# One accumulator row, two copies and five late weight pieces at the end of a decode-attention kernel

## Chip, cores and metric

The kernel runs on one core of a Trainium2 chip. The metric is device time in microseconds (us) for one execution; lower is better. Before the change three runs took 1010.38, 1010.63 and 1011.29 us, median 1010.63.

## What is computed

One query token attends to two caches, and a gate mixes the two results. All data is float32.

```python
def attention(x, k, v, wq, wo):          # x: [1, 448]; 16 query heads of 256; 8192 positions
    q = (x @ wq).reshape(16, 256)
    p = softmax(einsum("hd,hkd->hk", q, k) * 256 ** -0.5)
    return einsum("hk,hkd->hd", p, v).reshape(1, 4096) @ wo      # [1, 448]

g = sigmoid((x * gate_w).sum(-1))
out = g * attention(x, A_k, A_v, A_wq, A_wo) \
    + (1 - g) * attention(x, repeat(B_k, 2), repeat(B_v, 2), B_wq, B_wo)
```

A has 16 key/value heads, B has 8, each serving two query heads. The caches make up nearly all of the 432 MB that the kernel reads.

## The kernel before

**The stream.** The host lays all inputs into one array, `stream`, in the order in which they are used. `plan()` writes this order: a list of fills, each a list of loads, each a list of pieces (kind, number, offset, columns). A ring of three SBUF slots takes the fills in turn, and the loop at the end of the kernel issues the loads on SP's queue (L469) and calls `piece` for each piece. Most fills are one load of 7936 KB. The last ones are cut finer by hand: the last key/value tiles, then the last tile of values in three loads (`LAST_CUT`, 8, 4 and 4 rows), then the last set's output weights `wo` in four loads: 448 KB (head 3), 448 KB (head 0), 672 KB (head 1 and half of head 2), 224 KB (the other half of head 2).

**The work.** There are eight sets (`s` from 0 to 7). A set is three units: unit 2 is a B head with its two query heads, units 0 and 1 are two A heads. A unit is four tiles of 2048 positions. TensorE computes scores of units 2 and 1 (`scores`, L255); VectorE computes those of unit 0 (`scores_by_row`, L277 and L281). ScalarE takes the exponentials, and TensorE multiplies with the values (`attend`, L307). At a unit's end ScalarE and VectorE merge the two halves of its accumulator (`take`, L316 and L317), `combine` and `column` make its softmax weights (L337 to L366), and `project_o` (L372, copy L374) turns the result into columns.

**The output.** `YY[0]` is a PSUM tile that collects the output. For sets 0 to 6 `emit_set` (L381) multiplies each of the four heads of a set with its wo and adds it to row 0, 32, 64 or 96 by head, 448 columns wide. After set 6 `fold` copies the tile to SBUF (L387), takes a new one, clears it (L186) and sums the four rows into it (L391) by a column `any4` that has ones at these rows: from here on row 32g holds columns 112g to 112g + 111. `emit` (L398) adds a head of the last set in this form: two halves of the head (`e`) times four column blocks (`g`), eight matmuls of 112 columns. In the trace a float32 matmul is two instructions.

**The end.** The order is written out after the loop: project the last unit, (s, 1), then `emit` for (s, 2) head 0, (s, 1), (s, 2) head 1 and (s, 0), as the four wo loads come. VectorE copies rows by 112 columns (L483), and SP stores four pieces of 448 bytes (L484). The schedule is manual: each engine runs its instructions in the order of the program, and the framework sets the semaphores.

Of the kernel before, what the change touches and what calls it, by code (L numbers as in the profile page):

```python
# [7 lines left out]
F32 = mybir.dt.float32  # L8
BF16 = mybir.dt.bfloat16
AF = mybir.ActivationFunctionType  # L10
# [4 lines left out]
P = 128  # L15
D = 448
# [3 lines left out]
KF = D // P  # L20
KR = D - KF * P
NG = 4
YN = D // NG

NS = 8
ROWS = 16
# [10 lines left out]
BY_ROW = {(s, 0) for s in range(NS)}  # L37
LAST_CUT = [8, 4, 4]
HEAD_AT = {2: 0, 0: 2, 1: 3}
TILES = [((s, r), t) for s in range(NS) for r in UNITS for t in range(NT)]  # L40


# [4 lines left out]
def plan():  # L47

    size = {"xg": XG, "k": ROWS * DH, "v": ROWS * DH, "wq": WQ, "wo": 8 * D}
    per = len(UNITS) * NT  # L50
    n = len(TILES)
    items = []
    for i in range(n + LEAD):
        if i == 0:
            items += [("xg", 0), ("wq", 0)]
        if i < n:
            items.append(("k", i))
        if i >= LEAD:
            items.append(("v", i - LEAD))
        if i % per == 7 and i // per + 1 < NS:  # L60
            items.append(("wq", i // per + 1))
        if i % per == LEAD + 1 and i >= per:
            items.append(("wo", i // per - 1))
    loads, room = [[]], FULL
    last = [("v", n - 3), ("v", n - 2)]
    for kind, i in items[:items.index(last[0])]:
        at, left = 0, size[kind]
        while left:
            step = min(left, room) // ATOM[kind] * ATOM[kind]
            if step:  # L70
                loads[-1].append((kind, i, at, step))
            at, left, room = at + step, left - step, room - step * (kind != "xg")
            if left:
                loads.append([])
                room = FULL

    loads = [[x] for x in loads]
    x = loads[-2][0]
    loads[-2] = [x[:2], x[2:]]
    loads[-1] += [[(kind, i, 0, size[kind])] for kind, i in last]  # L80
    at, end = 0, []
    for c in LAST_CUT:
        end.append([("v", n - 1, at, c * DH)])
        at += c * DH

    for h, e, n in ((3, 0, 2), (0, 0, 2), (1, 0, 3), (2, 1, 1)):
        end.append([("wo", NS - 1, (2 * h + e) * D, n * D)])
    return loads + [end]


LOADS = plan()


@with_exitstack
def kernel(
# [5 lines left out]
    nc = tc.nc  # L101
    scale = DH ** -0.5

    const = ctx.enter_context(tc.tile_pool(name="const", bufs=1))
# [5 lines left out]
    ps_y = ctx.enter_context(tc.tile_pool(name="ps_y", bufs=1, space=PSUM))  # L110
# [3 lines left out]
    def heads(u):  # L114
        return 2 if u[1] == 2 else 1
# [35 lines left out]
    any4 = const.tile([P, 1], F32, name="any4")  # L151
# [33 lines left out]
    def clear(t, n):  # L185
        nc.tensor.matmul(t[:, :n], zero, zero[:, None, :n // 4].to_broadcast([P, 4, n // 4]), start=True, stop=False, skip_group_check=True)  # L186


    YY = [ps_y.tile([P, D], F32, name="Y")]
# [17 lines left out]
    ST, PR, O, GS, WR, SEL, OB, OC = ({} for _ in range(8))  # L207
# [103 lines left out]
    def take(u):  # L311

        o = O.pop(u)
        ob1 = small.tile([P, DH], F32, name="ob1", bufs=1)
        OB[u] = small.tile([P, DH], F32, name="ob", bufs=3)
        nc.scalar.activation(ob1, o[:, DH:], AF.Copy, scale=half[:, 1:2])  # L316
        nc.vector.scalar_tensor_tensor(OB[u], o[:, :DH], half[:, 0:1], ob1, op0=OP.mult, op1=OP.add)  # L317
# [50 lines left out]
    def project_o(u):  # L368
        M = heads(u)
        oc = ps_s.tile([P, 2, 2], F32, name="sm")  # L370
        for e in range(2):
            nc.tensor.matmul(oc[:, e, :M], OB[u][:, e::2], SEL[u][:, :M], start=True, stop=True)  # L372
        ocs = small.tile([P, 2, 2], F32, name="ocs", bufs=4)
        nc.vector.tensor_copy(ocs[:, :, :M], oc[:, :, :M])  # L374
        OC[u] = ocs
# [8 lines left out]
    def fold():  # L384

        yf = small.tile([P, NB * BLK], F32, name="px")
        nc.scalar.activation(yf[:, :D], YY[0], AF.Copy)  # L387
        YY[0] = ps_y.tile([P, D], F32, name="Y")
        clear(YY[0], YN)
        for g in range(NG):  # L390
            nc.tensor.matmul(YY[0][32 * g:32 * g + 1, :YN], any4, yf[:, g * YN:(g + 1) * YN], start=False, stop=False,  # L391
                             skip_group_check=True)

    def emit(u, m, last=False):
        for e in range(2):
            wt = LAST[HEAD_AT[u[1]] + m, e]
            for g in range(NG):
                nc.tensor.matmul(YY[0][32 * g:32 * g + 1, :YN], OC[u][:, e, m:m + 1], wt[:, g * YN:(g + 1) * YN],  # L398
                                 start=False, stop=(last and e == 1), skip_group_check=True)


    LAST, GW = {}, {}
# [3 lines left out]
    def wait(n, f, *args):  # L406
        todo.append([n, f, args])

    def tick():
        for t in todo:  # L410
            t[0] -= 1
        for t in [t for t in todo if t[0] <= 0]:
            todo.remove(t)
            t[1](*t[2])

    def piece(kind, i, at, view):
# [14 lines left out]
        elif kind == "k":  # L431
            u, t = TILES[i]
            if u in BY_ROW:
# [10 lines left out]
        elif kind == "v":  # L444
            u, t = TILES[i]
            n = view.shape[-1] // DH
            attend(u, t, at // DH, n, view.rearrange("p (j d) -> p j d", d=DH))
            if at // DH + n == ROWS:
                if t == NT - 1:
                    take(u)  # L450
                    if u != TILES[-1][0]:
                        wait(1, project_o, u)
                if i >= len(TILES) - LEAD:
                    tick()
        elif kind == "wo" and i < NS - 1:
            emit_set(i, j0, view.rearrange("p (c n) -> p c n", c=n))
            if i == NS - 2 and j0 + n == 8:
                fold()
        else:
            for j in range(n):  # L460
                LAST[divmod(j0 + j, 2)] = view[:, j * D:(j + 1) * D]

    off = 0
    for fill in LOADS:
        buf = ring.tile([P, FULL + XG], F32, name="slot")
        c = 0
        for load in fill:
            n = sum(x[3] for x in load)
# [4 lines left out]
                c += x[3]  # L473
    assert not todo
    s = NS - 1
    project_o((s, 1))
    emit((s, 2), 0)
    emit((s, 1), 0)
    emit((s, 2), 1)
    emit((s, 0), 0, last=True)  # L480

    ys = const.tile([P, YN], F32, name="ys")
    nc.vector.tensor_copy(ys, YY[0][:, :YN])  # L483
    nc.sync.dma_start(out.rearrange("a b (g n) -> (a b g) n", g=NG), ys[::32, :])  # L484


_OUTS = [((1, 1, D), "float32")]
# [64 lines left out]
```

## Time and profile before

| what | value |
|---|---|
| median of three runs | 1010.63 us |
| profiled execution | 1010.95 us |
| its span, first to last instruction | 1009.2 us |
| TensorE matmul busy | 578.0 us (57%) |
| VectorE busy | 465.1 us (46%) |
| read from HBM | 432.02 MB, 428 GB/s over the span |
| mean granted TensorE clock | 0.773 |

The span is what the profiler saw of the program; the execution's time is 1.8 us longer. In the profile PE is TensorE's matmuls, PEld its weight loads, DVE VectorE, ACT ScalarE, SP the queue that issues the loads. Times in the trace are counted from the span's start. PEclk is the TensorE clock granted, as a share of 2.4 GHz; it is 1.00 or 0.50 at any moment. A share of busy time is an average over the span; what a change at the end is worth is read from the last microseconds.

### The profile page before, as it was taken

How to read it: one execution, taken by the hardware profiler on the slowest of the kernel's cores; microseconds unless marked ns; L12 is line 12 of the kernel's file. 1: busy time of each engine (PE TensorE's matmuls, PEld its weight loads, DVE VectorE, ACT ScalarE, POOL GpSimd, SP SyncE). 2: the span in 40 equal slices, each digit the busy share in tenths (PEclk: the TensorE clock that was granted, in tenths of full speed). 3: DMA queues.
4: the chain of work that ended last, by engine and by line, in shares of the span. 5: the costliest groups of instructions: out<-in, count | busy, mean ns of one | idle time of the engine just before them, and what ended most of it. 6: DMA issues, size and time to landing. Idle time of an engine off the chain costs nothing.

```text
span 1009.2 us, 7624 instructions
## 1 busy us (share of the span) xinstructions
PE 578.0 (57%) x3154; PEld 169.8 (17%) x3154; DVE 465.1 (46%) x732; ACT 90.0 (9%) x267; POOL 1.9 (0%) x10
## 2 busy tenths in 40 slices
PE   0846745565745655636646556645656537537557
PEld 0211211121211111112111111111211112111112
DVE  1486213961248521576215841248521585216851
ACT  0100100010100110001100001100110000101010
POOL 0000000000000000000000000000000000000000
PEclk9977877767777887867787777776886777777788
DMA  9999999999999999999999999999999999999997
GB/s 403 439 438 425 431 436 439 435 421 433 439 436 425 436 431 441 431 428 433 441 428 429 438 431 433 435 431 438 431 431 426 440 438 426 428 433 441 424 421 299
DMA packets 9114, 432.50 MB, mean 429 GB/s; under 512 B 1016, under 2 KB 1144, under 8 KB 1784
## 3 DMA queue, kind: packets, MB, share of 16 engines
q1 hardware_dynamic: 9080, 432.02, 99.1%
q8 instruction: 24, 0.39, 0.2%
q14 instruction: 10, 0.08, 0.0%
HBM read 432.02 MB, written 0.00 MB: 428 GB/s over the span
## 4 chain that ended last, share of the span: by engine, by line
DMA 71%; PE 14%; DVE 12%; ACT 2%; issue 1%; ACTq 0%; SPq 0%; DVEq 0%
DMA slot<-in_stream_dram 71%; PE o L307 6%; PE sc L255 5%; DVE sr L281 4%; DVE slot L277 4%; PE sm L220 2%; ACT px L264 1%; DVE mn L261 1%; DVE pr L267 1%; PE sm L237 0%; DVE pr L294 0%; ACT pxr L290 0%; ACT ew L345 0%; PE sm L361 0%; DVE st L262 0%
## 5 line engine op out<-in xcount | busy, mean ns | idle before, releaser
L307 PE MATMUL o<-slot,pr 128*32 128x512 f32 (+1 forms) x1536 | 349.9, 758 | 224.6 <-DMA slot<-in_stream_dram 224.6
L255 PE MATMUL sc<-slot,qb 128*32 128x512 f32 x1024 | 197.5, 715 | 104.7 <-DMA slot<-in_stream_dram 101.7
L261 DVE TENSOR_REDUCE mn<-sc 128x1 f32<-128x512 f32 x64 | 44.1, 690 | 325.7 <-PE sc L255 300.9
L277 DVE TENSOR_TENSOR slot<-slot,qa 128x4096 f32<-128x4096 f32 (+7 forms) x40 | 142.6, 3565 | 41.1 <-DMA slot<-in_stream_dram 41.0
L307 PEld LDWEIGHTS o<-slot,pr 128*32 128x32 f32 (+1 forms) x1536 | 80.0, 142 | 405.2 <-DMA slot<-in_stream_dram 252.8
L281 DVE TENSOR_REDUCE sr<-slot 128x16 f32<-128x4096 f32 (+7 forms) x40 | 142.7, 3567 | 1.4
L255 PEld LDWEIGHTS sc<-slot,qb 128*32 128x32 f32 x1024 | 46.3, 129 | 221.1 <-issue 126.1
L264 ACT ACTIVATE px<-sc,st 128x512 f32<-128x512 f32 x64 | 44.0, 687 | 408.5 <-DVE st L262 386.6
L267 DVE STREAM_TRANSPOSE pr<-px 128x512 f32<-128x512 f32 x64 | 45.6, 713 | 58.9 <-ACT px L264 58.9
L220 PE MATMUL sm<-slot,xz 128*32 128x512 f32 x128 | 45.7, 707 | 35.8 <-DVE xz L193 23.0
L290 ACT ACTIVATE pxr<-sr,st 128x16 f32<-128x16 f32 x32 | 9.8, 308 | 373.6 <-DVE st L288 373.6
L372 PE MATMUL sm<-sel,ob 128*128 128x1 f32 (+1 forms) x96 | 17.5, 287 | 37.3 <-DVE ob L317 37.3
L317 DVE SCALAR_TENSOR_TENSOR ob<-o,half,ob 128x256 f32<-128x256 f32 x24 | 11.3, 470 | 44.0 <-ACT ob L316 44.0
L372 PEld LDWEIGHTS sm<-sel,ob 128*128 128x128 f32 x96 | 15.5, 228 | 61.8 <-DVE ob L317 53.6
L220 PEld LDWEIGHTS sm<-slot,xz 128*32 128x32 f32 x128 | 11.1, 128 | 65.4 <-issue 27.8
L294 DVE TENSOR_TENSOR pr<-pxr,cols 128x256 f32<-128x256 f32 x32 | 13.6, 426 | 15.9 <-ACT pxr L290 15.9
L316 ACT ACTIVATE ob<-o,half 128x256 f32<-128x256 f32 x24 | 11.3, 469 | 49.5 <-PE o L307 49.5
L361 PE MATMUL sm<-ones,wr 1*128 1x1 f32 x48 | 9.7, 268 | 10.4 <-DVE wr L354 10.4
L237 PE MATMUL sm<-px,spread 64*128 64x256 f32 x16 | 6.6, 498 | 13.9 <-DVE es L347 13.9
L381 PE MATMUL Y<-slot,ocs 128*1 128x448 f32 x112 | 13.4, 595 | 0.0
L361 PEld LDWEIGHTS sm<-ones,wr 1*128 1x128 f32 x48 | 7.8, 203 | 32.8 <-issue 28.1
L264 ACT ACTIVATION_READ_ACCUMULATOR px<-sc,st 128x1 f32 x64 | 12.3, 193 | 0.0
(73 smaller groups left out, 142.4 us busy)
## 6 DMA issues: line engine op xcount, KB each, us to landing
slot<-in_stream_dram SPq DMA_DIRECT2D x50, 7936.0 KB, 42.6
slot<-in_stream_dram SPq DMA_DIRECT2D x1, 7940.0 KB, 22.0
slot<-in_stream_dram SPq DMA_DIRECT2D x1, 4864.0 KB, 41.0
slot<-in_stream_dram SPq DMA_DIRECT2D x2, 2048.0 KB, 25.3
slot<-in_stream_dram SPq DMA_DIRECT2D x1, 3072.0 KB, 29.9
slot<-in_stream_dram SPq DMA_DIRECT2D x1, 1280.0 KB, 20.8
slot<-in_stream_dram SPq DMA_DIRECT2D x1, 1024.0 KB, 24.2
slot<-in_stream_dram SPq DMA_DIRECT2D x2, 512.0 KB, 25.5
```

What stands on the lines that cost most here:

```text
L220: nc.tensor.matmul(q[BLK * a:BLK * (a + 1), :], xz[:, c if c < KF else KF + a, :], w[:, j, :], start=(c == 0), stop=(c == KF), skip_group_ ...
L255: nc.tensor.matmul(sc[32 * g:32 * (g + 1), :], qb[:, e, at:at + 32], kt[:, j, :], start=(e == 0), stop=(e == 1), skip_group_check=True)
L261: nc.vector.tensor_reduce(mn, sc, axis=AX.X, op=OP.min)
L264: nc.scalar.activation(px, sc, AF.Exp, bias=st[:, 0, t:t + 1], scale=-1.0, accum_out=st[:, 1, t:t + 1])
L267: nc.vector.transpose(pr.rearrange("p (q r k) -> p q k r", r=BLK, k=2), px.rearrange("p (q k c) -> p q k c", c=BLK, k=2))
L277: nc.vector.tensor_tensor(kt, kt, QA[u][:, None, :].to_broadcast([P, n, DH]), op=OP.mult)
L281: nc.vector.tensor_reduce(sc[:, j0:j0 + n], kt, axis=AX.X, op=OP.add)
L294: nc.vector.tensor_tensor(pr, px[:, :, None, :].to_broadcast([P, ROWS // 2, NG * NT, 2]), cols[:, t].rearrange("p g r -> p (g r)")[:, None ...
L307: nc.tensor.matmul(O[u][w * g:w * (g + 1), :], pr[:, j // 2, :w], vt[:, j - j0:j - j0 + 2, :], start=(t == 0 and j < 2 * P // w), stop=(t ...
L361: nc.tensor.matmul(cl, WR.pop(u).rearrange("p c x m k -> p (c x m k)"), ones[:1, :], start=True, stop=True)
L372: nc.tensor.matmul(oc[:, e, :M], OB[u][:, e::2], SEL[u][:, :M], start=True, stop=True)
L381: nc.tensor.matmul(YY[0][32 * h:32 * h + 1, :], OC[s, r][:, e, m:m + 1], wt[:, j, :], start=False, stop=(s == NS - 2 and e == 1), skip_gro ...
```

## The change

The output tile after `fold` is one row of 448 columns. `fold` sums the four rows with one matmul and does not clear; `emit` is one matmul of 448 columns for each half of a head. The last wo comes in five loads, heads 0, 1, 2 and the two halves of head 3, so that the last unit's weights are behind the others. Head 0 is multiplied before the last unit is projected, and the last unit's head last. ScalarE and VectorE copy one half of the row each, and the store is one piece of 1792 bytes. In `plan()` the rest of one tile of values (1280 KB) and the next tile (2048 KB) become one load.

```diff
+WO_CUT = [2, 2, 2, 1, 1]
@@ plan
-    loads[-1] += [[(kind, i, 0, size[kind])] for kind, i in last]
+    (v1, v2) = [(kind, i, 0, size[kind]) for kind, i in last]
+    loads[-1][0].append(v1)
+    loads[-1].append([v2])
@@
-    for h, e, n in ((3, 0, 2), (0, 0, 2), (1, 0, 3), (2, 1, 1)):
-        end.append([("wo", NS - 1, (2 * h + e) * D, n * D)])
+    at = 0
+    for c in WO_CUT:
+        end.append([("wo", NS - 1, at, c * D)])
+        at += c * D
@@ fold
-        YY[0] = ps_y.tile([P, D], F32, name="Y")
-        clear(YY[0], YN)
-        for g in range(NG):
-            nc.tensor.matmul(YY[0][32 * g:32 * g + 1, :YN], any4, yf[:, g * YN:(g + 1) * YN], start=False, stop=False,
-                             skip_group_check=True)
+        YY[0] = ps_y.tile([1, D], F32, name="Y")
+        nc.tensor.matmul(YY[0], any4, yf[:, :D], start=True, stop=False, skip_group_check=True)
@@ emit
-            for g in range(NG):
-                nc.tensor.matmul(YY[0][32 * g:32 * g + 1, :YN], OC[u][:, e, m:m + 1], wt[:, g * YN:(g + 1) * YN],
-                                 start=False, stop=(last and e == 1), skip_group_check=True)
+            nc.tensor.matmul(YY[0], OC[u][:, e, m:m + 1], LAST[HEAD_AT[u[1]] + m, e],
+                             start=False, stop=(last and e == 1), skip_group_check=True)
@@ the end
+    emit((s, 2), 0)
     project_o((s, 1))
-    emit((s, 2), 0)
-    emit((s, 1), 0)
     emit((s, 2), 1)
-    emit((s, 0), 0, last=True)
-
-    ys = const.tile([P, YN], F32, name="ys")
-    nc.vector.tensor_copy(ys, YY[0][:, :YN])
-    nc.sync.dma_start(out.rearrange("a b (g n) -> (a b g) n", g=NG), ys[::32, :])
+    emit((s, 0), 0)
+    emit((s, 1), 0, last=True)
+
+    ys = const.tile([1, D], F32, name="ys")
+    nc.scalar.activation(ys[:, D // 2:], YY[0][:, D // 2:], AF.Copy)
+    nc.vector.tensor_copy(ys[:, :D // 2], YY[0][:, :D // 2])
+    nc.sync.dma_start(out.rearrange("a b n -> (a b) n"), ys)
```

## Rows read from the trace of the kernel before

**Rows 1.** The page: the span, and the chain of waits by engine.
```profile
span 1009.2 us, 7624 instructions
...
DMA 71%; PE 14%; DVE 12%; ACT 2%; issue 1%; ACTq 0%; SPq 0%; DVEq 0%
```

**Rows 2.** The chain of waits, last 6 us: start us, us, what.
```profile
985.98 18.74 DMA slot<-in_stream_dram
1004.72 0.04 issue
1004.76 1.58 PE Y L398 x32
...
1006.37 0.27 DVE ys L483
```

**Rows 3.** Timeline, 1000.8 to 1008: start us, us, instruction, count, idle before.
```profile
1000.86 1.05 PE L307 MATMUL o<-slot,pr 128*32 128x512 f32 x4 [0.20 <-DMA slot<-in_stream_dram]
1002.02 0.47 ACT L316 ACTIVATE ob<-o,half 128x256 f32<-128x256 f32 x1 [8.31 <-PE o L307]
1002.52 0.48 DVE L317 SCALAR_TENSOR_TENSOR ob<-o,half,ob 128x256 f32<-128x256 f32 x1 [4.27 <-ACT ob L316]
...
1003.06 0.63 PE L372 MATMUL sm<-sel,ob 128*128 128x1 f32 x4 [1.15 <-DVE ob L317]
...
1003.62 0.95 PE L398 MATMUL Y<-slot,ocs 128*1 128x112 f32 x32
...
1006.67 0.66 SPq L484 DMA_DIRECT2D out_dram<-ys  x1
```

**Rows 4.** First and last wo load: timeline of SP, issues (KB, us to landing).
```profile
975.43 0.43 SPq L469 DMA_DIRECT2D slot<-in_stream_dram  x1
slot<-in_stream_dram SPq DMA_DIRECT2D x1, 448.0 KB, 26.5
...
990.88 0.33 SPq L469 DMA_DIRECT2D slot<-in_stream_dram  x1
slot<-in_stream_dram SPq DMA_DIRECT2D x1, 224.0 KB, 14.4
```

**Rows 5.** Timeline of TensorE's weight loads, L381 and L220; L381's matmul durations, ns.
```profile
932.17 0.12 PEld L381 LDWEIGHTS Y<-slot,ocs 128*1 128x1 f32 x4 [0.25 <-issue]
932.55 0.12 PEld L381 LDWEIGHTS Y<-slot,ocs 128*1 128x1 f32 x4 [0.25 <-issue]
...
836.83 0.17 PEld L220 LDWEIGHTS sm<-slot,xz 128*32 128x32 f32 x1 [0.68 <-issue]
837.68 0.12 PEld L220 LDWEIGHTS sm<-slot,xz 128*32 128x32 f32 x1 [0.68 <-issue]
...
838.55 0.14 PEld L220 LDWEIGHTS sm<-slot,xz 128*32 128x32 f32 x2 [0.29 <-issue]
838.98 0.14 PEld L220 LDWEIGHTS sm<-slot,xz 128*32 128x32 f32 x2 [0.29 <-issue]
...
L381 PE MATMUL Y<-slot,ocs x112: 537/538/952, 180.1 to 933.0; 128*1 128x448 f32 x112
```

**Rows 6.** Stretches: us, TensorE busy (count), granted clock, DMA share, GB/s.
```profile
998.30:1001.90 3.60, 3.16 (x16) 1.00 0.74 291
1001.90:1003.06 1.16, 0.01 (x2) 1.00 0.58 235
...
1004.95:1006.32 1.37, 1.37 (x32) 0.50 0.00 0
```

**Rows 7.** Timeline of TensorE: the last values but one, a column, the fold.
```profile
989.49 3.64 PE L307 MATMUL o<-slot,pr 128*32 128x512 f32 x32
...
995.82 1.92 PE L307 MATMUL o<-slot,pr 128*32 128x512 f32 x16 [2.65 <-DMA slot<-in_stream_dram]
997.68 0.38 PE L361 MATMUL sm<-ones,wr 1*128 1x1 f32 x2
...
934.39 0.37 PE L391 MATMUL Y<-px,any 128*1 128x112 f32 x8
```

**Rows 8.** Copies: ScalarE's durations by line (ns min/median/max); VectorE behind ScalarE, timeline.
```profile
L239 ACT ACTIVATE qa<-sm x8: 383/383/384, 32.6 to 847.3; 128x256 f32<-128x256 f32 x8
...
L387 ACT ACTIVATE px<-Y x1: 543/543/543, 933.7 to 933.7; 128x448 f32<-128x448 f32 x1
...
931.35 0.24 DVE L347 TENSOR_TENSOR es<-ew,sm 1x16 f32<-1x16 f32 x2 [0.55 <-ACT ew L345]
```

More of the change, by code (lines that the diff above doesn't have):

```diff
@@ L22 @@
 NG = 4
-YN = D // NG
 NS = 8
@@ L387, in fold @@
         nc.scalar.activation(yf[:, :D], YY[0], AF.Copy)
-        YY[0] = ps_y.tile([P, D], F32, name="Y")
-        clear(YY[0], YN)
-        for g in range(NG):
-            nc.tensor.matmul(YY[0][32 * g:32 * g + 1, :YN], any4, yf[:, g * YN:(g + 1) * YN], start=False, stop=False,
-                             skip_group_check=True)
+        YY[0] = ps_y.tile([1, D], F32, name="Y")
+        nc.tensor.matmul(YY[0], any4, yf[:, :D], start=True, stop=False, skip_group_check=True)
     def emit(u, m, last=False):
         for e in range(2):
-            wt = LAST[HEAD_AT[u[1]] + m, e]
-            for g in range(NG):
-                nc.tensor.matmul(YY[0][32 * g:32 * g + 1, :YN], OC[u][:, e, m:m + 1], wt[:, g * YN:(g + 1) * YN],
-                                 start=False, stop=(last and e == 1), skip_group_check=True)
+            nc.tensor.matmul(YY[0], OC[u][:, e, m:m + 1], LAST[HEAD_AT[u[1]] + m, e],
+                             start=False, stop=(last and e == 1), skip_group_check=True)
     LAST, GW = {}, {}
```

## Prediction

> **What bounds the kernel now.** I read the page first. Its chain of waits gives 71% of 1009.2 us to loads of the one input stream [rows 1]: for nearly the whole span the work is the 432 MB stream, and the change takes no byte from it. So only the end can move, and I read the chain over the last microseconds. It ends in three steps: the 672 KB load of wo lands at 1004.72, TensorE multiplies until 1006.34, VectorE copies until 1006.64 [rows 2]. Then the timeline of the same stretch, for what stands ahead of these: the last values' matmuls (1000.86), ScalarE and VectorE merge that accumulator (1002.02 and 1002.52), the last unit is projected (1003.06), two heads are multiplied at once (1003.62, 32 instructions in 0.95), and at 1006.67 the store is issued, 2.5 before the span ends [rows 3]. TensorE waits twice in it: to 1003.06 for the merge, to 1004.76 for a load. The change redraws this stretch of 8 us. The first wo load, 448 KB, is issued at 975.43 and lands 26.5 later, at 1001.93; the last, 224 KB, at 990.88 and lands 14.4 later, at 1005.28 [rows 4].
>
> **Part 1: one row in place of four.** Now a head's product is eight matmuls of 112 columns in four row blocks of the accumulator (rows 0, 32, 64, 96). Afterwards it is two matmuls of 448 columns, all in row 0. A float32 matmul is two instructions in the trace. What one block alone is worth is read from the weight loads, which go one per matmul instruction [rows 5]. Where the work has four blocks (L381, 448 columns), four instructions start every 0.38 us (932.17 to 932.55). Where L220 works on two blocks, two start every 0.43 us with 512 columns (838.55 to 838.98). Where L220 starts with one block alone, one starts per 0.85 us (836.83 to 837.68), at half the clock. So a block takes an instruction of 512 columns per 0.43 us at 2.4 GHz, whatever the others do; 448 columns take 0.375. The blocks run beside each other, and the change gives up three of them. A head then costs 2 x 2 x 0.375 = 1.50 us at 2.4 GHz; now two heads take 0.95 together.
>
> **Part 2: the order at the end.** Head by head, with the landings of part 3:
> - Row (s,2) head 0 goes ahead of the projection. Its 448 KB land at 1001.93, as the first 448 KB of wo do now [rows 4]; the start follows a landing by 0.04 [rows 2]: 1001.98 to 1003.48.
> - The projection, now started at 1003.06 by the merge [rows 3], finds TensorE taken until 1003.48: 0.42 late. Its four instructions hold TensorE for 0.56 (1003.06 to 1003.62), so to 1004.04. The copy behind it is not urgent: its head is last now.
> - Then (s,2) head 1, (s,0) and (s,1), 1.50 each: 1005.54, 1007.04, 1008.54. The last instruction starts 0.375 before that and lasts 0.54 [rows 5]: the result is there at 1008.70.
> - Now it is there at 1006.34, so TensorE ends 2.36 later.
>
> All of this is at 2.4 GHz. In the profiled execution the clock fell to half at 1004.95 [rows 6], after TensorE had stood idle for nearly all of 1.16 us (1001.90 to 1003.06) and waited again before 1004.76. Afterwards those gaps are filled: from 1001.98 on only the 0.56 of the projection is not long matmuls. In 998.30 to 1001.90, busy for 3.16 of 3.60 with short waits, the clock held at 1.00 [rows 6]. I take the full clock to the end.
>
> **Part 3: the loads.** The last wo is 448, 448, 448, 224, 224 KB in place of 448, 448, 672, 224. The bytes are the same, so the pieces land at about 1001.93, 1003.0, 1004.1, 1004.7 and 1005.3. The old wait for the 672 KB goes, and what is late next is TensorE itself: each head's load has landed before its turn (the last by 1005.3, the turn is 1007.04). SP gets one load fewer before these and one more behind. Each late load is issued when an older one lands (985.98, behind the landing at 985.96 [rows 2]); the last would move from 990.88 to the landing that starts TensorE at 995.82 [rows 7], still 9.5 us before its bytes are due and 11 us before TensorE asks. Nothing is queued behind it on SP but the store. Cost 0; if the cover failed, it would add only what it lands after 1007.0.
>
> The 1280 KB and 2048 KB loads of values become one, which lands at 990.9 when the second does now. TensorE reaches these values at 989.49 [rows 7], so some 1.4 us shift at most, behind which stand the matmuls that wait for 995.82 anyway and the column at 997.68 [rows 7]; its consumer is the projection after 1003. Cost 0.
>
> The fold at 934.39 becomes one matmul of 448 columns, two instructions, 0.75 + 0.16, against a clearing matmul and 0.37 [rows 7]: below 0.5 us, 20 us before the next wait that counts. Cost 0.
>
> **Part 4: copy and store.** Now VectorE copies 112 columns in 0.27 [rows 2]. Afterwards ScalarE and VectorE copy 224 each, from one accumulator. ScalarE starts 0.11 behind a matmul's end (1001.91 to 1002.02 [rows 3]) and takes 256 columns in 0.383, 448 in 0.543 [rows 8], so 224 in 0.36. VectorE lies between 0.27 for 112 and 0.48 for 256 [rows 3], so 0.43. Side by side they end at 1008.70 + 0.11 + 0.36 = 1009.17; one after the other (VectorE starts 0.03 after ScalarE's end, 1002.49 to 1002.52 [rows 3]) at 1009.63. No row shows the two reading one accumulator at once for independent results. The nearest is two ScalarE instructions and the VectorE products from the same accumulator: VectorE starts at 931.35, behind both, though the first product needs only the first [rows 8]. I take one after the other, and keep 1009.17 as the low end. The Trainium skill, PSUM — Partial Sum Buffer, section on bank collisions, speaks against the halves too: two engines that read the same bank and 32-partition quadrant collide, so a dependency is put between ScalarE and VectorE. By that rule the second engine only adds a hand-over; without it the copy would end 0.46 earlier. The trace agrees as far as that one row goes.
>
> The store is one piece of 1792 bytes for four of 448. No other store exists here; loads of 448 and 224 KB are issued in 0.43 and 0.33 [rows 4] and the present store in 0.66 [rows 3]. The bounds are 0.33 either way; I take 0, the present row.
>
> **Sum.** The copy ends at 1009.63 against 1006.64: +2.99. The profiled execution took 1010.95 (span 1009.2), so 1013.94. The median of the three runs is 0.32 lower, 1010.63; with it 1013.6. Of the 2.99, TensorE makes 2.36, the copies 0.63. Changes below 0.2% (2.0 us) are about what can't be told from none.
>
> **Rivals.**
> - *A lone block streams a column per clock* (not slower). Place: TensorE from 1003.62 on. 448 columns at 2.4 GHz are 0.187, a head 0.75. Head 0 ends at 1002.73, the projection stays at 1003.06, the others run 1003.62 to 1004.37 and 1005.12, the last head's second half (landed 1005.28) ends near 1005.9, result at 1006.05; the copies take it to 1006.98, +0.34: 1011.0, no change. With E for a head the result comes at 1002.70 + 4E when TensorE is the bound; slower by 0.2% begins at E = 1.26. For it: single instructions look alike whether blocks overlap or not. Against it: the lone 0.85 and the pairs at 0.43 [rows 5]. TensorE: Matmul & The Clock Gate, § Back-to-back issue gap, in the Trainium skill has N/2.4 + 2.5 ns per matmul, which is this rival; by it the sum would be 1011, and the trace disagrees, 0.43 for 512 columns.
> - *The clock falls at 1004.95 as it does now* (slower still). By then 0.90 of 4.50 us of the last three heads is done; the other 3.60 take 7.2. +3.6: 1017.2. For it: it fell there [rows 6]. Against: the idle time ahead of the fall is gone.
> - *The copies run side by side and the store is quicker*: 0.46 to 0.79 less, 1012.8 to 1013.2; same sign.
> - *The pieces do what they seem cut for*, only 224 KB left to multiply when the stream ends: that is the first rival, and needs a head below 0.8 us.
>
> **How the numbers follow.** The forecast, with either way of copying, 0.80, range 1012.6 to 1014.6. The lone block at full rate 0.08 (1011.0 to 1011.5). The half clock 0.08 (up to 1017.5). Something that shortens the end beyond these, 0.04. The range 1011.8 to 1015.6 leaves out most of the last three. Slower by over 0.2%: 0.76 of the forecast's 0.80 plus 0.08, so 0.84; within 0.2%: 0.04 + 0.07, so 0.12 with a part of the last; faster: 0.04.
>
> **What would show it.** In the changed kernel's timeline L398's successor should have 16 instructions of 128x448, four per head, 0.375 apart, from about 1002 to 1008.5 counted from a stream that ends as now, with the projection between the first head and the rest; no wait for a load in the chain's last 4 us, but TensorE for some 4.5 us; granted clock 1.00 there; VectorE's copy starting behind ScalarE's. The forecast is wrong if instructions of one head start closer than 0.3 us at full clock, if the last wait of the chain is a load, or if the clock is 0.50 in the last heads.

## The result and the profile after

The changed kernel takes 1013.99 us (median of 6 runs, 1013.87 to 1014.10) against 1010.54 us (6 runs, 1010.38 to 1011.29): 3.45 us more, a ratio of 1.0032 with a 95% interval of 1.0022 to 1.0042. The forecast was 1013.6 us, slower. The profiled execution took 1014.02 us, its span is 1012.2.

The chain of waits of the changed kernel, its end (start us, us, what), answers [rows 2]:

```profile
976.66 24.83 DMA slot<-in_stream_dram
1001.49 0.04 issue
1001.53 1.05 PE o L310 x4
1002.59 0.03 issue
1002.61 1.66 PE Y L396 x4
1004.27 0.56 PE sm L375 x4
1004.84 4.62 PE Y L396 x12
1009.45 0.02 issue
1009.48 0.36 ACT ys L481
1009.83 0.02 issue
1009.86 0.38 DVE ys L482
```

Before, the last wait for the stream ended at 1004.72, and 1.9 us of work followed. Now the chain leaves the stream at 1001.49, where the last values land, and 8.7 us of work follow, nearly all of it TensorE's: no wo load is waited for behind the first. The timeline of the same stretch answers [rows 3]:

```profile
1002.61 0.09 PEld L396 LDWEIGHTS Y<-slot,ocs 128*1 128x1 f32 x2 [0.93 <-DMA slot<-in_stream_dram]
1002.61 1.66 PE L396 MATMUL Y<-slot,ocs 128*1 128x448 f32 x4
...
1004.21 0.63 PE L375 MATMUL sm<-sel,ob 128*128 128x1 f32 x4
...
1004.77 4.67 PE L396 MATMUL Y<-slot,ocs 128*1 128x448 f32 x12
...
1009.48 0.35 ACT L481 ACTIVATE ys<-Y 1x224 f32<-1x224 f32 x1 [6.31 <-PE Y L396]
1009.86 0.38 DVE L482 COPY ys<-Y 1x224 f32<-1x224 f32 x1 [4.82 <-ACT ys L481]
1010.26 0.32 SPq L483 DMA_DIRECT2D out_dram<-ys  x1
```

One head of four instructions, the projection, three heads with twelve instructions in all, two copies one behind the other, the store. The weight loads give the rate, one instruction per 0.38 us where [rows 5] has four:

```profile
1005.14 0.08 PEld L396 LDWEIGHTS Y<-slot,ocs 128*1 128x1 f32 x1 [0.29 <-issue]
1005.52 0.08 PEld L396 LDWEIGHTS Y<-slot,ocs 128*1 128x1 f32 x1 [0.29 <-issue]
1005.90 0.08 PEld L396 LDWEIGHTS Y<-slot,ocs 128*1 128x1 f32 x1 [0.29 <-issue]
```

And the stretches with their granted clock (us, busy and count of TensorE, its weight loads, VectorE, ScalarE and GpSimd, then clock, DMA share, GB/s), where [rows 6] has 0.50 at the end:

```profile
1004.95:1006.32 1.37, 1.37 (x5) 0.30 (x4) 0.09 (x1) 0.00 (x0) 0.00 (x0) 1.00 0.02 9
1006.32:1009.10 2.78, 2.78 (x9) 0.54 (x7) 0.00 (x0) 0.00 (x0) 0.00 (x0) 1.00 0.00 0
```

TensorE is busy without a gap and keeps the full clock to the last head.

From profile to profile the span grows by 3.07 us, which divide like this (us from the span's start, then lengths in us):

| term | before | after | difference | forecast |
|---|---|---|---|---|
| first wo load lands | 1001.93 | 1002.57 | +0.64 | 0 |
| from there to the result | 4.41 | 6.87 | +2.46 | +2.36 |
| from the result to the end of the copies | 0.30 | 0.79 | +0.49 | +0.63 |
| from there to the end of the span | 2.53 | 2.01 | -0.52 | 0 |

The two large terms are those of the forecast. Two terms were taken as 0, +0.64 and -0.52, and nearly cancel; that they do is luck. A third difference lies in the base: the profiled execution of before is 0.41 above the median of these six runs, so that medians differ by 3.45 where the profiled executions differ by 3.07.

### The profile page after: what moved, and what is told of

It reads as the page before. It is cut to its first block, busy times and chain, and to the rows that moved or that the text cites. A ratio compares the mean times of both kernels' runs of the same rounds, so it can differ in the third digit from the quotient of the medians.

```text
span 1012.2 us, 7515 instructions
## 1 busy us (share of the span) xinstructions
PE 583.4 (58%) x3099; PEld 168.7 (17%) x3099; DVE 465.3 (46%) x732; ACT 90.8 (9%) x268; POOL 1.9 (0%) x10
## 4 chain that ended last, share of the span: by engine, by line
DMA 72%; PE 13%; DVE 12%; ACT 1%; issue 1%; SPq 0%; ACTq 0%; DVEq 0%
DMA slot<-in_stream_dram 72%; PE o L310 6%; PE sc L258 5%; DVE sr L284 5%; DVE slot L280 5%; PE sm L223 1%; ACT px L267 1%; DVE mn L264 1%; PE Y L396 1%; DVE pr L270 1%; PE sm L240 0%; ACT ew L348 0%; DVE pr L297 0%; ACT pxr L293 0%; PE sm L364 0%
```

## The experiments

The theory is that of the forecast: with one row block TensorE is the bound of the end. The rival is that the loads, their order or the copies cost the time.

**Four blocks put back.** The changed kernel's loads and order, with the old accumulator, copy and store:

```diff
...
-            nc.tensor.matmul(YY[0], OC[u][:, e, m:m + 1], LAST[HEAD_AT[u[1]] + m, e], ...)
+            for g in range(NG):
+                nc.tensor.matmul(YY[0][32 * g:32 * g + 1, :YN], OC[u][:, e, m:m + 1], wt[:, g * YN:(g + 1) * YN], ...)
...
-    nc.scalar.activation(ys[:, D // 2:], YY[0][:, D // 2:], AF.Copy)
-    nc.vector.tensor_copy(ys[:, :D // 2], YY[0][:, :D // 2])
+    nc.vector.tensor_copy(ys, YY[0][:, :YN])
...
```

> The changed kernel's loads and order at the end, with the four row blocks of 112 columns, the one VectorE copy and the store in four pieces put back. Theory (TensorE with one block bounds the end): a head costs 0.38 us again, so TensorE waits for the last load once more and has the result about 0.4 us behind its landing, where the kernel before has it 1.04 behind (at half clock for most of that): 1010.0 to 1010.6 us. Rival (the later pieces, the merged load or the order cost the time): stays near 1014.

Measured: 1010.54 us (11 runs), ratio 1.0 (0.9991 to 1.0009). With four blocks the loads and the order cost nothing; the 3.45 us go with the one row. The end of its chain of waits:

```profile
995.75 9.58 DMA slot<-in_stream_dram
1005.33 0.04 issue
1005.37 0.42 PE Y L402 x8
1005.79 0.02 issue
1005.81 0.28 DVE ys L487
```

Here the finer cut of the last loads does what it can: TensorE waits for the very last piece and has the result 0.46 behind its landing. That is 0.6 earlier than in the profile of before, where the result came 1.04 behind the last landing at half clock, yet no run time shows it: the medians are equal. Why not is taken up under the second profiles.

**Two blocks.** As four_blocks with two blocks of 224 columns and a store of two pieces of 896 bytes (`YB = 2`, `YN = D // YB`, loops over `range(YB)`).

> As four_blocks with two row blocks of 224 columns, copied by VectorE alone and stored in two pieces of 896 bytes. Theory (a block takes an instruction per 0.375 us of 448 columns, blocks run beside each other): a head costs 0.75, the result comes about 0.75 behind the last landing, the copy takes 0.38: 1010.3 to 1011.0 us, some 0.4 above four_blocks less what a store in fewer pieces gives back. Rival (a lone block already streams at full rate, the loss is elsewhere): no difference from one row, near 1014 less the copies.

Measured: 1010.67 us (11 runs), 0.13 above four blocks. Timeline:

```profile
1001.77 0.93 PE L403 MATMUL Y<-slot,ocs 128*1 128x224 f32 x8
...
1002.87 0.63 PE L377 MATMUL sm<-sel,ob 128*128 128x1 f32 x4 [0.17 <-DVE ob L322]
...
1003.43 2.44 PE L403 MATMUL Y<-slot,ocs 128*1 128x224 f32 x24
...
1005.92 0.39 DVE L488 COPY ys<-Y 128x224 f32<-128x224 f32 x1 [2.22 <-PE Y L403]
1006.34 0.63 SPq L489 DMA_DIRECT2D out_dram<-ys  x1
```

A head of eight instructions takes 0.93 with its tail, where one block takes 1.66 for four and four blocks take 0.56 for sixteen, in four_blocks:

```profile
1001.92 0.56 PE L402 MATMUL Y<-slot,ocs 128*1 128x112 f32 x16
```

The cost is that of the longest block, as the theory has it. The result stands 0.73 behind the last landing (1005.16 to 1005.89), where 0.75 was expected, against 0.46 with four blocks, so two blocks lose next to nothing.

**One row alone.** The kernel before with its own loads and order, and the one row with its copies and store.

> The kernel before with its own loads and order, and only the one row, its two copies and the single store of the change. Theory (TensorE with one block bounds the end): the projection starts at 1003.06 again and four heads of 1.50 us follow one behind the other, 1003.62 to 1009.62, about 1 us later than in the changed kernel, which puts one head ahead of the projection: about 1015 us. Rival (loads and order cost the time): 1010.5 to 1011.2.

Measured: 1015.16 us (5 runs, 1015.12 to 1015.65), ratio 1.0045 (1.0033 to 1.0058). Timeline:

```profile
1004.30 0.63 PE L372 MATMUL sm<-sel,ob 128*128 128x1 f32 x4 [1.16 <-DVE ob L317]
...
1004.86 6.17 PE L393 MATMUL Y<-slot,ocs 128*1 128x448 f32 x16
```

Its stretches (us, busy and count of TensorE, granted clock, DMA share, GB/s):

```profile
1004.90:1008.00 3.10, 3.10 (x10) 1.00 0.03 12
1008.00:1011.00 3.00, 3.00 (x9) 1.00 0.00 0
```

Sixteen instructions in 6.17, the forecast's 6.0 and a tail. So the loads and the order of the change together are worth 1.17 us (1015.16 to 1013.99) once the one row is there: the changed kernel runs a head (1002.61) while the last unit is merged (1002.69 to 1003.68), and here TensorE waits for the merge. With four blocks they are worth nothing.

**One copy.** The changed kernel with VectorE alone:

```diff
-    nc.scalar.activation(ys[:, D // 2:], YY[0][:, D // 2:], AF.Copy)
-    nc.vector.tensor_copy(ys[:, :D // 2], YY[0][:, :D // 2])
+    nc.vector.tensor_copy(ys, YY[0])
```

> The changed kernel with one VectorE copy of 448 columns in place of the two halves. Theory (the halves run one behind the other: ScalarE 0.35, hand-over, VectorE 0.38, 0.79 us behind the result in all): one copy of about 0.59 ends 0.63 behind the result, 0.15 us faster than the changed kernel, 1013.8. Rival (two halves are worth having because two engines share the work): 0.15 to 0.3 us slower than the changed kernel.

Measured: 1013.87 us (6 runs, 1013.68 to 1013.95), 0.12 below the changed kernel, with ranges that overlap. The timeline shows the same gain, one copy that ends 0.63 behind the result (1009.42) instead of 0.79:

```profile
1009.44 0.61 DVE L481 COPY ys<-Y 1x448 f32<-1x448 f32 x1 [4.44 <-PE Y L396]
1010.08 0.32 SPq L482 DMA_DIRECT2D out_dram<-ys  x1
```

**Two banks.** The row in two accumulators of 224 columns, the second in a buffer of the scores that is free by then.

```diff
...
+    def fold_rest():
+        YY.append(ps_sc.tile([P, NB * BLK], F32, name="sc")[:1, :D // 2])
+        nc.tensor.matmul(YY[1], any4, YF[0][:, D // 2:], start=True, stop=False, skip_group_check=True)
...
+            for b in range(2):
+                nc.tensor.matmul(YY[b], OC[u][:, e, m:m + 1], wt[:, b * (D // 2):(b + 1) * (D // 2)], ...)
...
-    nc.scalar.activation(ys[:, D // 2:], YY[0][:, D // 2:], AF.Copy)
+    nc.scalar.activation(ys[:, D // 2:], YY[1], AF.Copy)
...
```

> The changed kernel with the row in two accumulators of 224 columns in different banks (a head is four matmuls of 224 columns instead of two of 448; the sum of the second half's four rows is made while TensorE waits for the last values). Theory (ScalarE and VectorE take turns because both read one accumulator): now they copy side by side and end about 0.45 us behind the result instead of 0.79, so 0.3 to 0.4 us faster than the changed kernel, 1013.6; TensorE's time for a head stays 1.50. Rival (they take turns for another reason, the shared output tile or the engines): the times of the changed kernel, 1014.0, VectorE still starting behind ScalarE.

Measured: 1013.78 us (6 runs, 1013.62 to 1013.91), 0.21 below the changed kernel. Timeline:

```profile
1009.15 0.54 PE L402 MATMUL sc<-slot,ocs 128*1 128x224 f32 x2
...
1009.35 0.38 DVE L490 COPY ys<-Y 1x224 f32<-1x224 f32 x1 [4.09 <-PE Y L402]
1009.73 0.35 ACT L489 ACTIVATE ys<-sc 1x224 f32<-1x224 f32 x1 [6.33 <-PE sc L402]
```

VectorE no longer waits for ScalarE (`<-ACT ys` in the changed kernel, `<-PE Y` here), although ScalarE's copy stands first in the program; it copies the first half while TensorE still works on the second. So the turns came from the shared accumulator, not from the shared output tile or the engines. The Trainium skill, PSUM — Partial Sum Buffer, section on bank collisions, states such a dependency between ScalarE and VectorE for one bank and quadrant, and the trace agrees: 0.79 from the result to the end of the copies with one accumulator, 0.38 with two. Whether the bank or the tile makes the dependency, this run does not tell. Nor does it show two copies side by side: VectorE is done at 1009.73, when ScalarE starts. The gain in the copies is that one half is taken before the result is complete. The median gained less than these 0.41, 0.21; in this profile the first wo load landed 0.21 later than in that of the changed kernel.

**Second profiles.** What was open was 3.45 measured against 2.99. Two theories: the profiled execution of before was untypical (A), or the stream itself ends later in kernels with one row (B). Each of three kernels was run again unchanged.

> The kernel before unchanged, a second profile. Open is why the measured difference is 3.45 us where the sum gave 2.99. Theory A (the profiled execution against which the sum was made was untypical: half clock over its last 1.4 us, worth 0.65): here the clock stays at 1.00 until TensorE is done, the second half of L398 takes 0.95 instead of 1.55, and the result comes 0.95 behind the landing of the 672 KB load instead of 1.6. Theory B (the stream ends later in kernels with one row): the first wo load lands 0.5 us or more earlier here than in after_again. Both can hold.

> The changed kernel unchanged, a second profile. Theory A: first wo landing to the end of the last copy 7.7 us as in its first profile, landing within 0.3 us of before_again. Theory B: landing 0.5 us or more later than in before_again and four_again.

> four_blocks unchanged, a second profile. Theory A: the first wo load lands at about the time it does in after_again, within 0.3 us. Theory B: 0.5 us or more earlier than there.

Measured: 1011.23, 1014.01 and 1010.65 us, one execution each. In after_again the first wo load lands at 1002.56, 0.54 later than in before_again and 0.57 later than in four_again. The table takes two readings from the profiles so far: when TensorE starts on the last values, 0.04 behind their landing, and how much later than in the first profile of before two 7936 KB loads landed, those that land there at 136.65 and 832.93.

| kernel | one row | last values start, us | the two loads against before, us |
|---|---|---|---|
| before | no | 1000.86 | 0 / 0 |
| before_again | no | 1000.95 | -0.30 / -0.30 |
| four_blocks | no | 1000.81 | -0.41 / -0.40 |
| four_again | no | 1000.92 | -0.40 / -0.40 |
| two_blocks | no | 1000.66 | -0.90 / -0.96 |
| after | yes | 1001.53 | -0.47 / +0.02 |
| after_again | yes | 1001.52 | -0.01 / +0.49 |
| one_copy | yes | 1001.52 | -0.06 / +0.43 |
| one_row_only | yes | 1002.09 | +0.06 / +0.48 |
| two_banks | yes | 1001.77 | +0.04 / +0.50 |

Theory B holds: kernels with one row get their last values 0.6 to 1.2 later. The right column shows where: not only at the end, but little by little along the span. Where a profile stands at 137 us differs by up to 0.5 even between two profiles of one kernel, so only the change from there to 833 us is read: each kernel with one row falls back by 0.4 to 0.5 us, each other one by less than 0.1, although up to 930 us all of them have the same instructions. In after_again the loads between stand at +0.18 (361 us) and +0.25 (550 us). Theory A failed as it was put: the clock fell in the second execution of before too, at 1004.99, and 1011.23 is well above the median. Most of the other executions of before took 1010.3 to 1010.7; whether their clock holds was not seen, so why four_blocks is no faster than before stays open.

**The place in SBUF.** What the kernels with one row share before 930 us is where things lie. The output tile is allocated ahead of the ring of the stream; it has grown from 112 to 448 columns, so the ring lies 1344 bytes further on in every partition. Two kernels tell this apart: four_shifted is four_blocks with the ring where the changed kernel has it, one_row_shifted the changed kernel with the ring where the kernel before has it. In both, the small buffers behind the ring move with it.

```diff
-    ys = const.tile([P, YN], F32, name="ys")
+    ys = const.tile([P, D], F32, name="ys")[:, :YN]
```

> four_blocks with the output tile declared 448 columns wide instead of 112 (the first 112 are used): only the place of everything behind it in SBUF moves, by 1344 bytes a partition, the ring of the stream with it, to where the changed kernel has it. Open is why the stream's loads land some 0.6 us later at the end in all profiles of kernels with one row. Theory (the ring's place in SBUF makes the stream slower by 0.07%): 1011.1 to 1011.3, loads drifting later by some 0.5 us from 137 to 927 us against four_blocks. Rival (something else of the one row): 1010.5, no drift.

```diff
+    pad = const.tile([P, D // 4], F32, name="pad")
+    nc.vector.memset(pad[:1, :1], 0.0)
...
-    ys = const.tile([1, D], F32, name="ys")
+    ys = small.tile([P, NB * BLK], F32, name="px")[:1, :D]
```

> The changed kernel with its output row in a buffer that exists already and an unused tile of 448 bytes a partition ahead of the ring: the ring lies in SBUF where the kernel before has it, all else as in the changed kernel. Theory (the ring's place): 0.6 us faster than the changed kernel, 1013.3 to 1013.5, no drift of the loads against the kernel before. Rival: 1014.0, the drift stays.

Measured: four_shifted 1011.20 us (11 runs), 0.66 above four_blocks; one_row_shifted 1013.43 us (8 runs, 1013.30 to 1013.55), 0.56 below the changed kernel, whose six runs lie above all of these. Both comparisons are with runs of an earlier series. In the series of these two the kernel before took 1010.75, 0.2 more than earlier; four_shifted is 0.45 above it, with a ratio of 1.0005 (0.9996 to 1.0014) that does not by itself tell the two apart. The spans scatter less: 1009.0 to 1009.4 in four_shifted against 1008.6 to 1009.0 in four_blocks and 1008.5 to 1009.4 in the kernel before of the same series (medians 1009.3, 1008.6 and 1008.8), and 1011.5 to 1011.8 in one_row_shifted against 1012.1 to 1012.3 in the changed kernel. The traces are clearer still. The loads near 137 and 833 us stand at -0.42 and +0.06 in four_shifted, a drift of 0.48, and at -0.89 and -0.85 in one_row_shifted, next to none; the last values start at 1001.39 and 1000.85. Both as the theory has it. The chain of waits of one_row_shifted:

```profile
1001.96 1.67 PE Y L398 x4
1003.62 0.56 PE sm L377 x4
1004.18 4.62 PE Y L398 x12
1008.80 0.02 issue
1008.82 0.35 ACT px L483
1009.18 0.02 issue
1009.20 0.38 DVE px L484
```

It is the chain of the changed kernel, 0.65 earlier at every step. Its wo loads land at 1001.91, 1003.04, 1004.21, 1004.78 and 1005.36, close to the times that the forecast had for them; in the changed kernel each is 0.56 to 0.66 later.

## Why the prediction was right, step by step

- **One block in place of four** (part 1): right. 0.376 us an instruction, one at a time, against 0.375 forecast; four_blocks, two_blocks and one_row_only show that this cost goes with the longest block, not with the loads, the order or the copies. The first rival, a lone block at a column per clock, is out: it needed 0.187. The rule that spoke for it, a gap of N/2.4 + 2.5 ns between matmuls in the Trainium skill's TensorE: Matmul & The Clock Gate, § Back-to-back issue gap, would give 0.19 for each instruction of 448 columns, an estimate; the trace disagrees, the rows of this float32 kernel show twice that.
- **The order at the end** (part 2): right but for 0.09. The projection started 1.59 behind the first head's start (1002.61 to 1004.21) where 1.50 was counted, so it does not follow a head's last instruction as closely as another head does. From the first wo landing to the result 6.87, forecast 6.77.
- **The clock**: the level was right, the reason is not shown. The granted clock is 1.00 until the last head in all six profiles of kernels with one row, so the second rival, 1017.2, is out. The forecast put the fall down to the idle time ahead of it, which the change fills. But in one_row_only TensorE stands idle for 1.16 before the projection, as in the kernel before, and the clock holds all the same. The kernel before waits once more, 0.19 before 1004.76, and one_row_only does not; whether that matters was not tried. What made the clock hold stays open, and to that extent the forecast was lucky here.
- **The loads** (part 3): right for what it says. The last load was issued at 996.48 and landed at 1005.92, 2.6 us ahead of its turn. The merged one landed at 991.57; TensorE stood 0.95 for it and had made that up when the next values came. The part did not ask where in SBUF the loads land. That is the missing term, 0.56 us by the medians and 0.64 between the profiles, the largest error in the sum.
- **The copies** (part 4): the way was right, one behind the other; the size 0.14 too high (0.93 from the result to the end, 0.79 measured): ScalarE started 0.04 behind the result, not 0.11, and VectorE took 0.38, not 0.43. The third rival held in one of its two parts: the store is quicker. Copies side by side no run shows; with two accumulators they end 0.41 earlier, one half ahead of the result.
- **The store** (part 4): mis-sized, 0 taken and 0.33 given as the bound, where it gave back 0.52. Of this, 0.34 lies in the issue on SP (0.66 before, 0.32 after, 0.63 with the two pieces of two_blocks). From the end of the copies to the end of the span, before, four_blocks and two_blocks take 2.5, the kernels with a store in one piece 2.0. Two pieces of 896 bytes are no better than four of 448, so it is the single piece, from one partition, that counts here. The Trainium skill, DMA: Bandwidth & Descriptors, section Specifications, gives 512 bytes as the least transfer for line rate; had that decided here, two_blocks would have shared the gain, and the trace does not show it, 2.5 with 896.
- **The base**: the sum was made against an execution 0.41 above the median and 0.32 was taken off, so 0.1 of the measured difference lies there.

With the ring in its old place the difference of the medians is 2.68 (1013.43 to 1010.75, the kernel before in the same series), against a forecast of 2.99. So the mechanism was right, and the closeness of 1013.6 to 1013.99 is in part luck: the quicker store made up for most of the later stream.

No version here beats the kernel before: four_blocks equals it, and the best with one row, one_row_shifted, is 0.26% slower (1.0026, 1.0016 to 1.0036).

## What to carry to other kernels

Here a float32 product with one row of output was bound by its one row block; cutting the columns over four blocks lets four of them run beside each other, and a single-piece store did not repay giving that up (0.52 against 2.46 us). Two engines that copy halves of one accumulator were no quicker than one engine alone (0.79 against 0.63 behind the result). Before a cut of the last loads is counted as a gain, ask which engine is behind when they land: with a result 3.5 us behind the last landing, no piece of the stream was waited for. And when a tile ahead of a streaming ring changes its size, measure the ring's place by itself. A gain or loss of half a microsecond is compared with the kernel before of the same series, and better in the traces.

## What was not expected of the hardware

The place of the ring in SBUF changes the rate of a 432 MB stream: with the ring 1344 bytes further on in each partition the loads of two kernels fall back by 0.5 us between 137 and 833 us, and the medians differ by 0.56 and 0.66, about 0.06%. The small buffers behind the ring moved too, and the two were not told apart. The chip is not the reason: on each of the three chips on which the experiments ran, one kernel shows the drift and another does not. In two_banks, 3136 bytes further on by its two tiles, the drift is as large; in two_blocks, 448 bytes further on, there is none. Why, and which places are good, was not settled.
